# Putting off the last addition of seven units in a dynamic convolution that feeds a maxout layer

## The chip, the core and the metric

The kernel runs on one core of a Trainium2 chip. The metric is the device time of one execution in microseconds (us); the median of three executions stands for the kernel. TensorE (PE) multiplies matrices into PSUM, VectorE (DVE) and ScalarE (ACT) work elementwise, GpSimd (POOL) and SyncE (SP) here mostly issue transfers. Each engine works through its own list of instructions in order, and waits on semaphores for the others.

## What is computed

Two layers follow each other. The first is a convolution whose seven weights are different for every position and head, and are a softmax of an input; the second is a maxout layer with an output projection.

```python
# x: 8 x 4160 x 192, weight_gen: 8 x 4160 x 8 heads x 7 taps
w = exp(weight_gen); w = w / sum(w, axis=-1)          # softmax over the 7 taps
y[b, s, h, :] = sum over k of w[b, s, h, k] * x[b, s - 6 + k, h, :]
# maxout on the 33280 rows of y: w1, w2 192 x 1024, w_out 1024 x 192
out = maximum(y @ w1, y @ w2) @ w_out
```

## The kernel before, in words

**Layout.** The 33280 positions lie as 128 partitions by 260 columns. `BATCHES` are 16 columns each (17 of them, the last of 4). A batch is worked in units: from column 32 on a unit is 8 columns, so batch b has a unit at offset 0 and one at offset 8. A unit is named here by its first column: unit 40 is batch 2, offset 8.

**Softmax.** The weights are exp(w - ln(sum exp w)), so nothing is divided. For each batch: `exp_sum` (ACT, line 162) takes exponents into `e_t`; `red` (DVE, 180) sums over the taps; `ln` (ACT, 186) takes the logarithm; `shift` (DVE, 191) subtracts it from the generated weights in place; `weights` (ACT, 202) takes the exponent again, each value doubled, as bfloat16 in `en_t`.

**Convolution.** For a unit, `mul` (DVE, 218) makes all seven products in one instruction, 128x10752, into its half of the one tile `m_t`. `adds` sums them in three levels: 4608 elements (248), 3072 (254), and the last addition of 1536 (260), which writes `y_t`. Levels two and three read what the level before has written. `beside` is called ahead of each level: on the units at offset 0 it cuts the next batch's `shift` into three parts, on those at offset 8 it puts two halves of a later batch's `red` ahead of levels one and two. Units from column 200 to 239 make the last addition in two halves.

**Around the unit.** `transpose(u)` has SP issue a transposing transfer (273) of `y_t` into `yt`. Results that are ready to be stored (512) are held in a list and issued on SP behind the next transposition. On POOL a copy of one value of `yt` into `gate` (281) makes the queue wait for the transposition; behind it POOL issues loads: for a unit at offset 8 the next x of two batches on and its halo (133, 154), for one at offset 0 the second half of the next batch's x and the weights of three batches on (133, 115).

**Maxout.** max(a, b) is a + relu(b - a), so `hid_tile` (PE, 373) multiplies `yt` by w2 - w1, `relu` (ACT, 383) moves that from PSUM to `rd_t`, and the output is `rd_t` times w_out (PE, 413) plus `yt` times the product of w1 and w_out (PE, 426), both into the same PSUM bank; `evac` (ACT, 498) copies it to `o_t`. Work goes by groups of three tiles (a tile is one eighth of a unit's hidden width), with two or four finished columns to each group in turn. `relay` lets one half of PE's output go behind the other by a wait on ACT's list (476).

**What sets the order.** The order is written out by hand. `hidden` walks a group; `steps` then calls `softmax_steps` and, for each tile, `extra`. `softmax_steps` takes ACT's softmax steps from the table `due`, by tile number; `AT` overrides single entries: ('l', c, 0) is the logarithm of batch c, 'W' are weights, 'X' is `exp_sum`. A step of a long kind can be moved to the next group; a logarithm is done in its group. `extra` has DVE's part: at a batch's tile 0 `mul(b + 1, 0)`, at tile 0 or 5 `adds(b + 1, 0)` with the shift of batch b + 2; at tile 8 `mul(b + 1, 8)`, at 8 or 13 `adds(b + 1, 8)` with the sums of batch b + 3. `wrap_mask` (ACT, 150) clears a part of the halo near the end of the work.

Of the kernel before, what the change touches and what calls it, by code (L numbers as in the profile page):

```python
# [13 lines left out]
ALU = mybir.AluOpType  # L14
# [3 lines left out]
def _sub(base: bass.AP, off: int, dims):  # L18
    ap = [list(base.ap[0])] + [[int(s), int(c)] for s, c in dims]
    return dataclasses.replace(base, offset=base.offset + off, ap=ap)  # L20
# [3 lines left out]
def kernel(  # L24
# [9 lines left out]
    nc = tc.nc  # L34

    B, S, D = x.shape
    H, K = weight_gen.shape[2], weight_gen.shape[3]
    F = moe_w1.shape[1]
    P = 128
# [11 lines left out]
    BATCHES = [(c, min(16, CPP - c)) for c in range(0, CPP, 16)]  # L51
    NB = len(BATCHES)


    def pieces(b):
        n = BATCHES[b][1]
        at, done = [], 0
        for w in (4, 4, 4, 4) if b < 2 else (8, 8) if n == 16 else (n,):
            at.append((done, w))
            done += w  # L60
        return at
# [37 lines left out]
    wg_ts, xb_ts, e_ts, s_ts, en_ts, y_ts, yt_ts = {}, {}, {}, {}, {}, {}, {}  # L99

    m_t = pm.tile([P, K * 16 * D], BF16, name="m_t")
# [20 lines left out]
    def x_at(b, o):  # L122

        c = BATCHES[b][0] + o
        key, at = (b, o) if c < LAST - 8 else ("wrap", 0) if c < LAST else (NB - 2, 8)
        if key not in xb_ts:
            xb_ts[key] = pxb.tile([P, (16 + PAD) * D], BF16, name="xb_t", tag="xb")
        return xb_ts[key], at * D
# [19 lines left out]
    def wrap_mask():  # L148
        halo = xb_ts["wrap"][:, 0:PAD * D]
        nc.scalar.activation(out=halo, in_=halo, func=AF.Copy, scale=msk[:, 0:1])  # L150
# [13 lines left out]
    def part(b, i, of):  # L164

        n = BATCHES[b][1]
        h0, h1 = n * i // of * H, n * (i + 1) // of * H
        return slice(h0, h1), h0 * K, [[K, h1 - h0], [1, K]]
# [4 lines left out]
    def sums(b, hs):  # L173

        at = BATCHES[b][0] * H - (0 if b < FIRST else s_parts[0].shape[-1])
        return s_parts[b >= FIRST][:, at + hs.start:at + hs.stop]

    def red(b, i=0, of=1):
        hs, at, ap = part(b, i, of)
        nc.vector.reduce_sum(out=sums(b, hs), in_=_sub(e_ts[b], at, ap), axis=AX.X)  # L180
# [7 lines left out]
    def shift(b, i=0, of=1):  # L188
        hs, at, ap = part(b, i, of)
        w_t = _sub(wg_ts[b], at, ap)  # L190
        nc.vector.tensor_tensor(out=w_t, in0=w_t, in1=_sub(s_ts[b], hs.start, [[1, hs.stop - hs.start], [0, K]]),  # L191
                                op=ALU.subtract)
# [15 lines left out]
    def mul(b, o):  # L208

        n = dict(pieces(b))[o]  # L210
        t, at = x_at(b, o)
        if n == 4 and b < 2:
            m_out = _sub(m_t, K * o * D, [[64, 2], [P, K * 6], [1, 64]])
            x_in = _sub(t, at, [[2 * D, 2], [D, K], [1, 2 * D]])
        else:
            m_out = m_t[:, K * o * D:K * (o + n) * D]
            x_in = _sub(t, at, [[D, K], [1, n * D]])
        return nc.vector.tensor_tensor(  # L218
            out=m_out, in0=x_in,
            in1=_sub(en_ts[b], o * WGC * 2, [[2, K * n * H], [0, G // 2], [1, 2]]),  # L220
            op=ALU.mult,
        )
# [11 lines left out]
    def in_halves(b, o):  # L234

        return 200 <= BATCHES[b][0] + o < 240

    def adds(b, o, first=False, beside=lambda i, of: None):


        w = dict(pieces(b))[o]
        n = w * D

        def taps(at, step, cnt):
            return _sub(m_t, K * o * D + at * n, [[step * n, cnt], [1, w * D]])

        beside(0, 3)
        nc.vector.tensor_tensor(out=taps(0, 1, 3), in0=taps(0, 1, 3), in1=taps(3, 1, 3), op=ALU.add)  # L248
        if first:
            return  # L250
        beside(1, 3)
        if b not in y_ts:
            y_ts[b] = py.tile([P, 16 * D], BF16, name="y_t", tag="y")
        nc.vector.tensor_tensor(out=taps(0, 2, 2), in0=taps(0, 2, 2), in1=taps(1, 5, 2), op=ALU.add)  # L254
        beside(2, 3)

        of = 2 if in_halves(b, o) else 1
        e = n // 2 // of
        for i in range(of):
            nc.vector.tensor_tensor(  # L260
                out=_sub(y_ts[b], o * D + i * 2 * e, [[64, 2], [P, e // 64], [1, 64]]),
                in0=_sub(m_t, K * o * D + i * e, [[n // 2, 2], [1, e]]),
                in1=_sub(m_t, K * o * D + 2 * n + i * e, [[n // 2, 2], [1, e]]), op=ALU.add,
            )

    def transpose(u):

        b, o, n = UNITS[u]
        yt = pyt.tile([P, 8 // 2 * 3 * P], BF16, name="yt", tag="yt")
        of = 2 if in_halves(b, o) else 1  # L270
        e = n * D // of
        for i in range(of):
            nc.sync.dma_start_transpose(
                out=yt[:, i * e:(i + 1) * e].rearrange("p (b t) -> p b t", t=P),
                in_=y_ts[b][:, o * D + i * e:o * D + (i + 1) * e],
            )
        yt_ts[u] = yt
        while held:
            held.pop(0)()

        nc.gpsimd.tensor_copy(out=gate, in_=yt[:, n * D - 1:n * D])  # L281
        c = b + 1 if o == 0 else b + 2
        if o == 8 and c < NB:
            load_x(c, 0, min(8, BATCHES[c][1]))
        if o == 0 and c < NB and BATCHES[c][1] > 8:
            load_x(c, 8, BATCHES[c][1] - 8)
        if o == 0 and b + 3 < NB:
            load_wg(b + 3, nc.gpsimd)
# [242 lines left out]
    OUTS, c = [[], [], []], 0  # L531
    for g in range(3, len(GROUPS)):
        most = 4 if g == 3 else 2 if GROUPS[g][1] == 2 or len(OUTS[-1]) == 4 else 4
        n = min(most, ready[g] - c)
# [92 lines left out]
    with tc.tile_pool(name="pstage", bufs=1) as pstage:  # L627
# [7 lines left out]
        for at, c, n in ((0, 2, PAD), (PAD, 8, 2), (PAD + 2, 10, 2)):  # L635
            nc.sync.dma_start(
                out=xs[:, at * D:(at + n) * D],
# [83 lines left out]
        for h in range(2):  # L721
# [4 lines left out]
            out=wo[:, :].rearrange("p (f d) -> p f d", d=D),  # L726
# [90 lines left out]
        sum_transpose(3)  # L817
        out_first_weights(OUTS[3])
        adds(1, 4, True)

    pout = work.enter_context(tc.tile_pool(name="pout", bufs=1))
# [8 lines left out]
    def end_of_1():  # L830
        mul(1, 12)
        shift(2)
        adds(1, 12, True)
# [87 lines left out]
    def rest_of_sum(u):  # L921
# [24 lines left out]
        ('l', 11, 0): 144,  # L946
        ('l', 12, 0): 162,
        ('l', 5, 0): 45,
    }
    due = {}  # L950
    for c in range(3, NB):
# [25 lines left out]
    def extra(t):  # L977

        u, k = TILES[t]
        b, o, n = UNITS[u]  # L980
        s = o + k

        if s == 0 and b + 1 < NB:
            mul(b + 1, 0)
        later = 0 if b < 4 else 5
        if s == later and b + 1 < NB:

            c = b + 1
            adds(c, 0, beside=lambda i, of: shift(c + 1, i, of) if c + 1 < NB else None)
        if s == 8 and b == NB - 3:  # L990
            wrap_mask()
        if s == 8 and b + 2 < NB:
            mul(b + 1, 8)
        if s == 8 + later and b + 2 < NB:
            adds(b + 1, 8, beside=lambda i, of: red(b + 3, i, 2) if b + 3 < NB and i < 2 else None)
        if k == n // 4 - 1 and 7 < u + 1 < NU:
            transpose(u + 1)

    def steps(g, tiles):

        if tiles:
            softmax_steps(g)
        for t in tiles:
            extra(t)
# [53 lines left out]
```

## Time and profile before

| | |
|---|---|
| median of 3 runs | 409.7 us (409.62, 409.70, 409.86) |
| the profiled execution | 410.27 us, its span from first to last instruction 408.5 us |
| PE matmul | busy 396.4 us, 97% of the span |
| PE weight load (PEld) | busy 316.5 us, 77% |
| DVE | busy 378.0 us, 93%, 235 instructions |
| ACT | busy 354.8 us, 87% |
| POOL | busy 78.7 us, 19% |
| DVE 218, 128x10752 | 28 times, 5751 ns each |
| DVE 248, 4608 elements | 28 times, 2551 ns each |
| DVE 254, 3072 elements | 28 times, 1752 ns each |
| DVE 260, 1536 elements | 23 times, 955 ns each |
| DVE 191, 280 or 336 values | 26 and 13 times, 444 and 502 ns |
| DVE 180, 448 to 64 values | 24 times, 613 ns |
| transposition, issue to landing | 34 times, median 3.7 us, 2.7 to 5.9 |

A line of the timeline gives the start in us from the span's start, the duration, engine, line and operation, the tile written and those read, and in brackets how long the engine had been idle and what ended that. A line of the chain gives start, length and what was running, followed back from the last instruction to whatever released it. DVE instructions overlap: the next begins some 0.08 us ahead of the end of the one before it, so what an instruction costs its engine is the distance from its start to the next start, not its duration.

### The profile page before, as it was taken

To read this page: it belongs to the slowest core of one execution; us is meant where nothing else is said; L and a number is where in the kernel's file an instruction comes from. 1 tells how busy PE (TensorE), PEld (TensorE's weight loads), DVE (VectorE), ACT (ScalarE), POOL (GpSimd) and SP (SyncE) were. 2 spreads that over 40 slices of the span, in tenths; PEclk is the share of its full clock that TensorE was granted. 3 is DMA by queue.
4 is the path that set the end of the run, shared out by engine and by line. 5 is a ranking of instruction groups with operands and counts; after the bars stand their busy time and mean duration, and the time that the engine had idled before them with its cause. 6 is when DMAs were issued, how large, how long until landed. Compare 5 with 4: busy or idle time off the path is not lost.

```text
span 408.5 us, 16132 instructions
## 1 busy us (share of the span) xinstructions
PE 396.4 (97%) x7369; PEld 316.5 (77%) x7369; DVE 378.0 (93%) x235; ACT 354.8 (87%) x420; POOL 78.7 (19%) x108
## 2 busy tenths in 40 slices
PE   7799999999999999999999999999999999999994
PEld 2589899777778777777877787777778777877794
DVE  6999999999999999999999999999999999999400
ACT  4889899999999988998989999899998899898771
POOL 1420122121212201222221122212212213110000
PEclk9999999999999999999999999999999999999999
DMA  8995588665767656775765676587468577936313
GB/s 252 251 196 139 153 151 198 146 159 153 194 92 230 187 109 140 219 190 107 219 183 105 161 207 181 106 215 192 100 161 214 142 107 220 178 80 155 116 66 119
DMA packets 65270, 66.32 MB, mean 162 GB/s; under 512 B 49585, under 2 KB 54321, under 8 KB 65200
## 3 DMA queue, kind: packets, MB, share of 16 engines
q1 hardware_dynamic: 56224, 40.54, 36.2%
q0 software_dynamic: 8832, 24.63, 29.8%
q8 instruction: 58, 0.95, 0.9%
q10 hardware_dynamic: 144, 0.10, 0.1%
q14 instruction: 12, 0.10, 0.1%
HBM read 37.33 MB, written 25.56 MB: 154 GB/s over the span
## 4 chain that ended last, share of the span: by engine, by line
PE 70%; DVE 17%; ACT 5%; DMA 3%; issue 1%; SPq 1%; POOL 0%; DVEq 0%; ACTq 0%; POOLq 0%
PE op_ps L413 31%; PE hd L373 29%; DVE m_t L218 8%; PE op_ps L426 6%; DVE m_t L248 4%; ACT rd_t L383 3%; DVE m_t L254 3%; PE hdp L373 2%; DMA ws1T<-in_moe_w_dram 2%; PE yps L318 2%; DVE y_t L260 1%; DMA xb_t<-in_x_dram 1%; DMA yt<-y_t 1%; DVE wg_t L191 1%; DVE s_rest L180 1%
## 5 line engine op out<-in xcount | busy, mean ns | idle before, releaser
L383 ACT ACTIVATE rd_t<-hd 128x1024 bf16<-128x1024 f32 (+1 forms) x206 | 234.5, 1188 | 26.0 <-PE hd L373 24.7
L413 PE MATMUL op_ps<-wo,rd_t 64*128 64x192 bf16 x4160 | 210.6, 243 | 0.1
L413 PEld LDWEIGHTS <-rd_t 64*128 64x128 bf16 x4160 | 180.8, 94 | 15.7 <-issue 0.3
L373 PE MATMUL hd<-yt,wd 64*128 64x512 bf16 (+1 forms) x1584 | 187.3, 360 | 0.4 <-ACT rd_t L383 0.3
L218 DVE TENSOR_TENSOR m_t<-xb_t,en_t 128x10752 bf16<-128x10752 bf16 (+1 forms) x35 | 181.5, 5192 | 0.1
L373 PEld LDWEIGHTS <-wd 64*128 64x128 bf16 x1776 | 94.2, 94 | 44.6 <-issue 4.0
L281 POOL CAST gate<-yt 128x1 f32<-128x1 bf16 x29 | 39.5, 1361 | 260.0 <-DMA yt<-y_t 260.0
L248 DVE TENSOR_TENSOR m_t<-m_t 128x4608 bf16<-128x4608 bf16 (+1 forms) x31 | 75.5, 2436 | 0.1
L498 ACT COPY o_t<-op_ps 128x384 f32<-128x384 f32 (+1 forms) x99 | 57.1, 588 | 12.5 <-PE op_ps L413 12.5
L426 PE MATMUL op_ps<-w,yt 64*128 64x192 bf16 x768 | 54.6, 243 | 0.1
L426 PEld LDWEIGHTS <-yt 64*128 64x128 bf16 x768 | 37.7, 94 | 16.3 <-issue 1.0
L254 DVE TENSOR_TENSOR m_t<-m_t 128x3072 bf16<-128x3072 bf16 (+1 forms) x29 | 50.0, 1724 | 0.1
L202 ACT ACTIVATE en_t<-wg_t 128x896 bf16<-128x896 f32 (+2 forms) x45 | 35.9, 820 | 0.2 <-DVE wg_t L191 0.2
L260 DVE TENSOR_TENSOR y_t<-m_t 128x1536 bf16<-128x1536 bf16 (+1 forms) x34 | 27.6, 825 | 0.5
L133 POOL DMA_DIRECT2D xb_t<-in_x_dram x34 | 18.3, 538 | 31.7 <-ACT rd_t L383 20.7
L191 DVE TENSOR_TENSOR wg_t<-wg_t,ln_t 128x280 f32<-128x280 f32 (+5 forms) x46 | 22.2, 482 | 0.4 <-ACT ln_t L186 0.3
L383 ACT ACTIVATE rd_t<-hdp 128x1024 bf16<-128x1024 f32 x16 | 16.3, 1037 | 1.6 <-PE hdp L373 1.6
L162 ACT ACTIVATE e_t<-wg_t 128x896 f32<-128x896 f32 (+2 forms) x18 | 16.3, 903 | 1.4 <-DMA wg_t<-in_weight_gen_dram 1.4
L488 DVE COPY o_last<-op_ps 128x192 f32<-128x192 f32 x1 | 0.4, 358 | 18.1 <-ACT o_last L488 18.1
L180 DVE TENSOR_REDUCE s_rest<-e_t 128x64 f32<-128x448 f32 (+2 forms) x27 | 16.3, 604 | 0.0
L373 PE MATMUL hdp<-yt,wd 64*128 64x256 bf16 x192 | 13.8, 270 | 2.3 <-ACT rd_t L383 2.0
L318 PE MATMUL yps<-ident,m_t 64*128 64x64 bf16 x600 | 12.1, 190 | 1.1 <-issue 0.6
(54 smaller groups left out, 88.6 us busy)
## 6 DMA issues: line engine op xcount, KB each, us to landing
out_dram<-o_t SPq DMA_DIRECT2D x22, 768.0 KB, 4.9
xb_t<-in_x_dram POOLq DMA_DIRECT2D x30, 384.0 KB, 5.0
out_dram<-o_t SPq DMA_DIRECT2D x20, 384.0 KB, 3.1
wg_t<-in_weight_gen_dram POOLq DMA_DIRECT2D x13, 448.0 KB, 5.8
xb_t<-xb_t POOLq DMA_DIRECT2D x15, 288.0 KB, 5.2
xb_t<-in_x_dram POOLq DMA_DIRECT2D x4, 192.0 KB, 5.9
xs<-in_x_dram SPq DMA_DIRECT2D x1, 576.0 KB, 3.7
yt<-y_t SPq DMA_TRANSPOSE x34, 3.7
```

Source lines behind the costliest of these rows:

```text
L191: nc.vector.tensor_tensor(out=w_t, in0=w_t, in1=_sub(s_ts[b], hs.start, [[1, hs.stop - hs.start], [0, K]]), op=ALU.subtract)
L202: nc.scalar.activation(out=_sub(en_ts[b], (o * WGC + j * N * K) * 2, [[2 * N, K], [2, N], [1, 2]]), in_=_sub(wg_ts[b], (o * H + j * N) * K ...
L218: return nc.vector.tensor_tensor(out=m_out, in0=x_in, in1=_sub(en_ts[b], o * WGC * 2, [[2, K * n * H], [0, G // 2], [1, 2]]), op=ALU.mult,)
L248: nc.vector.tensor_tensor(out=taps(0, 1, 3), in0=taps(0, 1, 3), in1=taps(3, 1, 3), op=ALU.add)
L254: nc.vector.tensor_tensor(out=taps(0, 2, 2), in0=taps(0, 2, 2), in1=taps(1, 5, 2), op=ALU.add)
L260: nc.vector.tensor_tensor(out=_sub(y_ts[b], o * D + i * 2 * e, [[64, 2], [P, e // 64], [1, 64]]), in0=_sub(m_t, K * o * D + i * e, [[n // ...
L281: nc.gpsimd.tensor_copy(out=gate, in_=yt[:, n * D - 1:n * D])
L373: nc.tensor.matmul(hid_out(t, f, j), lhsT=wd_at(j, s, f // 4, f % 4 * P, P), rhs=_sub(yt_ts[u][half(j), :], (s + j) % 3 * P, [[3 * P, w // ...
L383: relu_of[t0] = nc.scalar.activation(out=rd[:, k * 1024:(k + n) * 1024], in_=hd[:, at:at + n * 1024], func=AF.Relu)
L413: return nc.tensor.matmul(op_out(c), lhsT=rd[half(r), k * 1024 + at:k * 1024 + at + P], rhs=wo[half(r), f * D:(f + 1) * D], start=start, s ...
L426: nc.tensor.matmul(op_out(c + j), lhsT=yt_ts[u][half(j), (3 * i + (s + j) % 3) * P:(3 * i + (s + j) % 3 + 1) * P], rhs=w10[half(j), s * D: ...
L498: nc.scalar.copy(out=_sub(o, c % 24 * D, [[D, len(qs)], [h * D, 2], [1, D]]), in_=_sub(tile_, at + (qs[0] - p) * D, [[D, len(qs)], [512, 2 ...
```

## The change

For the seven units named in `PUT_OFF`, `adds` does not issue the last addition but keeps it in a list; `last_add`, called right behind each `mul` in `extra`, issues it behind the next unit's product. The places at which `beside` puts parts of `shift` or `red` change with it. Place 0 (between product and first addition) falls away where a put-off addition now stands there; place 2 (ahead of the last addition) falls away where the unit's own last addition is put off. The step is cut into as many parts as there are places left. Three logarithms, of batches 10, 14 and 15, are listed one group sooner, at tiles 127, 193 and 208 instead of 130, 196 and 212.

```diff
+    PUT_OFF = (32, 40, 48, 64, 72, 80, 88)
+    last_adds = []
+
+    def put_off(b, o):
+        return BATCHES[b][0] + o in PUT_OFF
+
-    def adds(b, o, first=False, beside=lambda i, of: None):
+    def adds(b, o, first=False, beside=lambda i, of: None, after=False):
...
-        beside(0, 3)
+        places = [i for i, there in enumerate((not after, True, not put_off(b, o))) if there]
+
+        def beside_at(i):
+            if i in places:
+                beside(places.index(i), len(places))
+
+        beside_at(0)
         nc.vector.tensor_tensor(out=taps(0, 1, 3), in0=taps(0, 1, 3), in1=taps(3, 1, 3), op=ALU.add)
...
-        beside(1, 3)
+        beside_at(1)
...
         nc.vector.tensor_tensor(out=taps(0, 2, 2), in0=taps(0, 2, 2), in1=taps(1, 5, 2), op=ALU.add)
-        beside(2, 3)
...
+        beside_at(2)
+
+        def last():
+            of = 2 if in_halves(b, o) else 1
...
+        if put_off(b, o):
+            last_adds.append(last)
+        else:
+            last()
+
+    def last_add():
+        if last_adds:
+            last_adds.pop()()
...
+        ('l', 15, 0): 208,
+        ('l', 14, 0): 193,
+        ('l', 10, 0): 127,
...
             mul(b + 1, 0)
+            last_add()
...
-            adds(c, 0, beside=lambda i, of: shift(c + 1, i, of) if c + 1 < NB else None)
+            adds(c, 0, beside=lambda i, of: shift(c + 1, i, of) if c + 1 < NB else None, after=put_off(c - 1, 8))
...
             mul(b + 1, 8)
+            last_add()
...
-            adds(b + 1, 8, beside=lambda i, of: red(b + 3, i, 2) if b + 3 < NB and i < 2 else None)
+            adds(b + 1, 8, beside=lambda i, of: red(b + 3, i, min(of, 2)) if b + 3 < NB and i < 2 else None,
+                 after=put_off(b + 1, 0))
```

More of the change, by code (lines that the diff above doesn't have):

```diff
@@ L254, in adds @@
         nc.vector.tensor_tensor(out=taps(0, 2, 2), in0=taps(0, 2, 2), in1=taps(1, 5, 2), op=ALU.add)
-        beside(2, 3)
[L257 to L264, printed above, removed]
+        beside_at(2)
+        def last():
+            of = 2 if in_halves(b, o) else 1
+            e = n // 2 // of
+            for i in range(of):
+                nc.vector.tensor_tensor(
+                    out=_sub(y_ts[b], o * D + i * 2 * e, [[64, 2], [P, e // 64], [1, 64]]),
+                    in0=_sub(m_t, K * o * D + i * e, [[n // 2, 2], [1, e]]),
+                    in1=_sub(m_t, K * o * D + 2 * n + i * e, [[n // 2, 2], [1, e]]), op=ALU.add,
+                )
+        if put_off(b, o):
[5 more added lines that the diff above has]
+            last_adds.pop()()
     def transpose(u):
```

## The prediction, made before the changed kernel was run

> **What bounds the kernel now.** I read PE's waits first, then the chain that ended last, and then the periods in the timelines. The waits of PE, in us in total, times, longest:
>
> ```profile
> PE hdp L373 <- ACT rd_t L383: 2.0, 3, 0.9
> PE warm L689 <- DVE ident L666: 1.6, 1, 1.6
> PE warm L689 <- DVE m_t L227: 0.7, 1, 0.7
> ...
> PE hd L373 <- ACT rd_t L383: 0.3, 1, 0.3
> PE warm L709 <- DVE wd L704: 0.3, 1, 0.3
> ```
>
> All of PE's waits for DVE are on lines of the opening, before 12.5 us. The change touches nothing before the subtraction at 47.15. Behind that PE never waits for DVE. Now the chain around the place where it leaves PE (start, length):
>
> ```profile
> 254.88 1.32 PE op_ps L413 x32
> ...
> 263.52 1.32 PE op_ps L413 x32
> ...
> 272.15 1.32 PE op_ps L413 x32
> ...
> 278.15 5.75 DVE m_t L218
> ...
> 348.56 1.29 SPq L273
> 349.94 3.43 DMA yt<-y_t
> 353.50 1.03 POOL gate L281
> 354.53 3.47 DMA xb_t<-in_x_dram
> 358.21 1.26 ACT xb_t L150
> ...
> 367.33 1.32 PE op_ps L413 x32
> ```
>
> The chain runs over DVE from 278 to 348, and that looks as if DVE set the end. PE's own beat says otherwise. The block of 32 matmuls comes back every 8.64 us (263.52 less 254.88; 272.15 less 263.52). From 272.15 to 367.33 are 95.18 us; eleven beats of 8.635 are 94.99. In the whole stretch that the chain gives to DVE, PE loses 0.2 us. Starts of single matmuls in the trace confirm it: from 48 us to the last group the only distances over 0.21 us are 0.51 at 79.25 (PE there waits for ACT; 0.06 is normal at this step), 0.43 at 360.75, and four of about 0.25, where 0.20 is normal. So PE bounds the kernel, with some 0.9 us of gaps behind 48 us.
>
> DVE is busy without a gap from 41 to 355 us but is not late. I counted 48 hidden matmuls a unit and set the first of each against the landing of its transposition: for units 32, 40, 48, 64, 72, 80, 88 `yt` lands 10.1, 10.5, 9.8, 8.3, 7.4, 7.6, 7.2 us before its use. The lead shrinks as DVE takes 23.67 us for 16 columns (products at 41.49 and 65.15) and PE 23.03 (16/6 of 8.635), down to 1.2 us at units 216 and 232, and never to nothing.
>
> **The change part by part.** The row lengths are distances from start to next start on DVE.
>
> Ten instructions go, as the lists of the two built kernels show (248 rows, 238 now). Subtraction: parts of 280, 280 and 336 cost 0.36 + 0.36 + 0.42 = 1.14; two of 448 cost 2 x 0.54 = 1.09 (row at 15.87, next start 16.41); one of 896 costs 1.01 (38.22 to 39.23). Units 32, 64 and 96 go from three parts to two, 3 x 0.05 = 0.15. Units 48 and 80 go to one part, 2 x 0.13 = 0.26. Sums: two halves cost 1.06 (58.97 to 59.50, twice), one whole 1.00 (40.49 to 41.49); units 40, 72, 88: 3 x 0.06 = 0.18.
>
> The second saving is a stall between two additions of which one reads the other:
>
> ```profile
> 50.34 1.75 DVE L254 TENSOR_TENSOR m_t<-m_t 128x3072 bf16<-128x3072 bf16 x1
> 52.01 0.50 DVE L191 TENSOR_TENSOR wg_t<-wg_t,ln_t 128x336 f32<-128x336 f32 x1
> ...
> 62.49 1.75 DVE L254 TENSOR_TENSOR m_t<-m_t 128x3072 bf16<-128x3072 bf16 x1
> 64.28 0.96 DVE L260 TENSOR_TENSOR y_t<-m_t 128x1536 bf16<-128x1536 bf16 x1
> ```
>
> With a subtraction behind it line 254 costs 1.67, with its reader right behind it 1.79. The 0.12 goes at units 40, 72, 88 (the next product stands there) and 56 (a half sum does): 4 x 0.12 = 0.48. DVE gains 0.15 + 0.26 + 0.18 + 0.48 = **1.07 us**, all of it by about 146 us.
>
> What this is worth to the end: PE waits for DVE nowhere, so nothing directly. The one place left is 0.24 us at 360.75 (0.43 less 0.20), where ACT is late because of `wrap_mask`. The profile says that the mask waited 0.19 us for a load that DVE's chain had delayed. But its own list says:
>
> ```profile
> L150 ACTq EVENT_SEMAPHORE  x3: 38/38/38, 358.0 to 358.1; - x3
> ```
>
> Three waits stand ahead of the mask, each 38 ns, minimum and maximum alike: none of them was held. They begin behind the relay of line 476, which PE releases at 357.87, and three steps of 0.076 are the 0.19. An earlier load moves nothing there: **0**.
>
> The delayed last addition. It now follows the next product (5.67 us to the next start), less what DVE has saved till then: `y_t` comes 5.6 us later at unit 32, 5.4, 5.3, 5.1, 4.9, 4.8 at the next five, 4.6 at 88. Leads of 10.1 to 7.2 us become 4.5 at unit 32, 3.2 at 64, 2.5 at 72, 2.6 at 88. The cover holds unless a landing grows by 2.5 us; the slowest in the trace took 5.9 against a median of 3.7, which is 2.2 more. Cost 0, bounds 0 and (2.5 us beyond the cover) what rival B works out; nothing can be gained here. On SP the stores held behind a transposition go with it, some 2 us late at most; the stores next issued are ready at 56.30, 69.64, 81.02 and 105.42, the transpositions now at about 59.0, 70.7, 82.4 and 105.9. `o_t` holds 24 columns, and a place comes round again after 24 columns, over 30 us: nothing waits.
>
> POOL's gate. It is a copy on POOL and does not get through while a product runs:
>
> ```profile
> 69.36 1.59 POOL L281 CAST gate<-yt 128x1 f32<-128x1 bf16 x1 [8.62 <-DMA yt<-y_t]
> ...
> 80.88 1.89 POOL L281 CAST gate<-yt 128x1 f32<-128x1 bf16 x1 [8.91 <-DMA yt<-y_t]
> ```
>
> The first ends at 70.95, the product that ran ends at 70.91; the second at 82.77, its product at 82.72. A gate that came during a sum over taps took 0.19 (153.78). In the changed order a transposition that lands 3.7 us behind its issue meets the second addition, and the gate ends with that one: about 64.1, 75.8, 87.0, 110.9, 122.5, 134.2, 146.1, some 4.5 us later than before. What is queued behind it on POOL: the x loads have 12 us and more until their product. The weight loads of batches 5 to 8 landed at 65.97, 90.42, 115.82, 136.54 and their exponents began on ACT at 76.90, 95.73, 122.52, 148.43: 10.9, 5.3, 6.7, 11.9 ahead. Less 4.5 the least is 0.8, with the slow landing of 7.2 us that this load had. No cost.
>
> [...]
>
> Logarithms. DVE comes 1.07 us earlier; those of batches 10, 14 and 15 ended 0.93, 0.67 and 1.25 us ahead of their subtraction (211.89 and 212.82; 306.89 and 307.56; 330.11 and 331.36), so as listed before two of them would have held DVE. A group sooner they end about 3 to 6 us earlier, behind their sums (204.58, 299.24, 323.05 less 1.07). ACT issues as many as before; 0.21 us moves to another group. The same pairing, logarithm then weights, stands at 113.88 and 114.09, and PE shows no gap there: 0, bounds plus and minus 0.2. The next tightest, weights of batch 11 (253.13 for a product at 254.49), has 1.36 against 1.07.
>
> **Sum.** The profiled execution took 410.27 (span 408.5 and 1.77 around it), 0.57 over the median. 410.27 - 0 = 410.27 in its terms, **409.7** for the median.
>
> **The rivals.**
>
> A, faster: DVE does pace the end, as the chain has it from 278 to 348, and the 1.07 us come off: 409.7 - 1.07 = 408.6. Against it stands the 0.2 us that PE lost there. [...] The beat of 8.64 speaks against it. 6%.
>
> B, slower: a gate does not get in between the second addition and the next product, which begins 0.08 us before the addition ends, or its transposition lands more than 4.9 us behind the issue. It then waits out a product, 5.7 us more. Place: units 64 to 88. At unit 64 the loads would go at 116.6 and 117.1; the weights land 5.8 (median) to 8.9 us (that load's row) later, 122.9 to 126.0, and the exponent due at 122.52 holds ACT, its relus and PE for 0.4 to 3.5. At unit 88 loads issued at 140.0 and 140.5 would run beside a transposition issued at 140.9; landing when they do (146.3 to 149.4) it would miss the use at 147.33 by up to 2.1. I take 1.1: 410.8. It decides at a landing 4.9 us behind the issue. For it: 4 of the first 9 transpositions took 4.5 to 5.9. Against it: the gate did get in at product and subtraction, which overlap by the same 0.08 us. 14%.
>
> C, a little: the mask did wait for its load, and 0.19 us go: 409.5. The three equal waits speak against it. 10%.
>
> **How the numbers follow.** Forecast 70%, 409.7. The kernel's measurement can tell about 0.2%, 0.8 us. Forecast and C lie within that: 80%; A is faster, 6%; B slower, 14%. The range 409.2 to 410.6 takes in forecast and C with the 0.2 us of the logarithms, and B's lower half.
>
> **What would show it.** DVE with 225 instructions; product of unit 240 at about 1.07 us before 348.80; that of unit 248, at 359.91, now waiting up to 0.6 for the mask, which stays near 358.2; gates at the seven times above; PE's beat 8.64 throughout and 0.43 again near 360.75. A gate near 116.6, or an exponent that waits for a load, means B; a gap gone at 360.75, C; a shorter beat after 272, A. A PE wait for `yt` in units 64 to 88 would make the prediction wrong.

## The result

The changed kernel takes 430.03 us (median of six executions, 426.93 to 431.11) where the kernel before took 410.13 beside it: a ratio of 1.0473, 95% interval 1.0435 to 1.0511. The profiled execution took 429.94 us, 19.7 more than that of before (spans 428.2 and 408.5). Line numbers from 248 on have moved: 248 is now 261, 254 is 267, 260 is 274, 273 is 296, 281 is 304, 373 is 396, 383 is 406, 413 is 436, 426 is 449, 476 is 499.

**Where it is lost.** First the slices of the span, 10.7 us each:

```profile
PE   7799999599999982999999999999999999999994
...
DVE  5999999599869966899999999999999999999500
...
POOL 1420209316901580222212212112212213130000
PEclk9999999879999995999999999999999999999999
```

PE has two holes, in the 8th slice (75 to 86 us) and the 16th (161 to 171), and the granted clock falls at both (digits 8 and 7 in the 8th and 9th slice, 5 in the 16th). DVE, which was full before, has holes as well. POOL, whose digits were 0 to 2 there, shows three blocks with peaks of 9, 9 and 8. From the 18th slice on the rows look as they did before: the beat in the chain (179.46, 188.09, 196.72, 205.36) is still 8.63 to 8.64 us. First uses of each unit's `yt` by PE come 7.45 us later at unit 48 (98.05, before 90.60), 7.9 at unit 88, 19.56 at unit 96 (178.63, before 159.07), and 19.55 for the rest. So 7.5 us go near 80, 0.4 on the way and 11.6 near 165.

The waits (us in total, times, longest):

```profile
ACT e_t L162 <- DMA wg_t<-in_weight_gen_dram: 19.1, 3, 12.6
...
PE op_ps L436 <- ACTq L499: 13.4, 2, 9.9
...
DVE m_t L218 <- DMA xb_t<-in_x_dram: 9.3, 2, 4.7
...
DVE m_t L218 <- DMA xb_t<-xb_t: 5.3, 1, 5.3
...
PE hd L396 <- ACT rd_t L406: 1.8, 1, 1.8
```

PE waits for ACT, ACT's exponents wait for the generated weights, and DVE's products wait for x. The chain tells in what order that came about, around the first hole (start, length):

```profile
59.46 3.75 DMA yt<-y_t
63.21 0.05 issue
63.27 11.55 POOL gate L304
...
76.69 5.10 DMA wg_t<-in_weight_gen_dram
...
81.82 0.02 ACT e_t L162
...
82.68 1.92 ACT rd_t L406 x2
84.60 0.04 issue
84.64 2.75 PE hd L396 x12
```

Read from the top: the transposition of unit 32 lands at 63.21; POOL's copy into `gate` begins and does not end; the load of batch 5's weights behind it is issued only at 76.69 and lands 5.1 us later; the exponent, the relus behind it and PE follow. The copy itself, and DVE at that time:

```profile
63.27 12.96 POOL L304 CAST gate<-yt 128x1 f32<-128x1 bf16 x1 [11.67 <-DMA yt<-y_t]
76.17 0.53 POOL L133 DMA_DIRECT2D xb_t<-in_x_dram  x1
76.69 0.55 POOL L115 DMA_DIRECT2D wg_t<-in_weight_gen_dram  x1
```

```profile
62.77 1.75 DVE L267 TENSOR_TENSOR m_t<-m_t 128x3072 bf16<-128x3072 bf16 x1
64.43 5.75 DVE L218 TENSOR_TENSOR m_t<-xb_t,en_t 128x10752 bf16<-128x10752 bf16 x1
70.10 0.95 DVE L274 TENSOR_TENSOR y_t<-m_t 128x1536 bf16<-128x1536 bf16 x1
70.97 2.55 DVE L261 TENSOR_TENSOR m_t<-m_t 128x4608 bf16<-128x4608 bf16 x1
73.44 1.08 DVE L191 TENSOR_TENSOR wg_t<-wg_t,ln_t 128x896 f32<-128x896 f32 x1
74.44 1.75 DVE L267 TENSOR_TENSOR m_t<-m_t 128x3072 bf16<-128x3072 bf16 x1
80.77 5.76 DVE L218 TENSOR_TENSOR m_t<-xb_t,en_t 128x10752 bf16<-128x10752 bf16 x1 [4.58 <-DMA xb_t<-in_x_dram]
```

A copy of one value a partition takes 12.96 us. It comes during a second addition, and five two-input instructions later, at 76.19, DVE has nothing to run: its next product (80.77) wants the x load that is queued behind the copy. 0.04 us later the copy ends. The copies of units 56 (99.80, 13.59 us) and 80 (143.54, 13.83 us) go the same way: that of 56 ends with the addition ahead of a sum over taps, that of 80 when DVE again has to wait for x.

At the second hole the weights of batch 8 go at 157.82 and take 11.03 us to land, beside two x loads and a transposition; their exponent waits 12.6 us and PE about 10. Behind the holes PE's matmuls stand about twice as far apart as usual (those of line 396 behind the first one 0.397 us where 0.197 is normal), and the granted clock is down: 0.50 from 84 to 89 us and from 162 to 171, 0.72 in the mean of either stretch of the changed kernel below (columns: stretch, length, busy us of PE, PEld, DVE, ACT and POOL, PEclk, DMA share, GB/s); the first fence is the kernel before:

```profile
80.00:92.00 12.00, 12.00 (x208) 9.23 (x206) 11.97 (x7) 11.03 (x14) 2.90 (x3) 1.00 0.58 140
...
157.00:175.00 18.00, 18.00 (x317) 14.04 (x314) 17.96 (x11) 16.31 (x19) 2.75 (x3) 1.00 0.78 207
```

```profile
80.00:92.00 12.00, 8.19 (x104) 6.22 (x106) 11.23 (x6) 7.30 (x8) 0.95 (x2) 0.72 0.57 156
...
157.00:175.00 18.00, 8.05 (x120) 6.01 (x116) 11.22 (x6) 6.08 (x7) 4.61 (x9) 0.72 0.73 114
```

Of the first 7.45 us, 5.5 are waits (distances of 3.88 and 2.04 less two normal ones of 0.2), and I put the other 1.9 down to the slow clock; of the 11.6 at the second, 10.0 and 1.6. The granted clock went to half near 83 us, behind the distance of 3.88, and near 162, inside one of 10. In the run of section 5 below, the granted clock was at half from 96.6 to 100.0 us (0.92 in the mean from 80 to 100) with nothing longer before it than distances of 0.88, 1.19 and 1.40 us between matmuls, within 4.5 us; there it took no single gap of 3.88 us.

DVE itself is as forecast: 225 instructions, 377.6 us busy (378.0 before).

### The profile page after: what moved, and what is told of

The parts are those of the page before. It is cut to its first block, busy times and chain, and to the rows that moved or that the text cites. A ratio compares the mean times of both kernels' runs of the same rounds, so it can differ in the third digit from the quotient of the medians.

```text
span 428.2 us, 16124 instructions
## 1 busy us (share of the span) xinstructions
PE 400.6 (94%) x7369; PEld 318.7 (74%) x7369; DVE 377.6 (88%) x225; ACT 354.9 (83%) x420; POOL 112.1 (26%) x108
## 4 chain that ended last, share of the span: by engine, by line
PE 67%; DMA 10%; DVE 7%; issue 6%; ACT 5%; POOL 3%; SPq 1%; ACTq 0%; DVEq 0%; POOLq 0%
PE op_ps L436 30%; PE hd L396 28%; PE op_ps L449 6%; DVE m_t L218 4%; DMA wg_t<-in_weight_gen_dram 4%; DMA yt<-y_t 3%; ACT rd_t L406 3%; POOL gate L304 3%; DMA xb_t<-xb_t 2%; PE hdp L396 2%; DMA ws1T<-in_moe_w_dram 2%; PE yps L341 1%; DVE m_t L261 1%; DVE m_t L267 1%; ACT o_t L521 0%
## 5 line engine op out<-in xcount | busy, mean ns | idle before, releaser
L304 POOL CAST gate<-yt 128x1 f32<-128x1 bf16 x29 | 73.2, 2523 | 240.2 <-DMA yt<-y_t 240.2
L191 DVE TENSOR_TENSOR wg_t<-wg_t,ln_t 128x280 f32<-128x280 f32 (+5 forms) x39 | 21.1, 541 | 0.4 <-ACT ln_t L186 0.3
```

## The experiments

The theory after the result, T1: POOL's copy reads SBUF and is kept out while DVE runs long two-input instructions without a break; all else follows from the late loads. The rivals: the put-off addition itself makes `yt` late; the merged subtractions and sums alone are enough; the logarithms; transfers that collide.

### 1. No copy, in the changed kernel and in the one before

```diff
-            nc.sync.dma_start_transpose(
+            turn = nc.sync.dma_start_transpose(
...
-        nc.gpsimd.tensor_copy(out=gate, in_=yt[:, n * D - 1:n * D])
+        tc.add_manual_dep(nc.gpsimd.nop().ins, turn.ins.name, SYNC, reason="loads behind the transposition")
```

> The changed kernel, but POOL no longer copies a value of yt: its first load behind a transposition waits for the transposition itself, so POOL reads nothing from SBUF. Theory 1 (the copy is shut out while DVE runs two-input instructions back to back; the weight loads behind it come late, their exponents hold ACT, and ACT holds PE): the three 13-us copies are gone, the loads of batches 5 and 8 are issued some 13 us sooner, no exponent waits over 1.5 us, and the time falls from 430.0 to 409.0 to 411.0. Theory 2 (the put-off addition itself makes yt late for PE): stays above 420. Theory 3 (transfers get in each other's way as soon as additions and loads are shifted against each other): between 412 and 425.

Measured: 409.87 us, ratio to the kernel before 0.9999 (0.9988 to 1.0009). The whole loss is gone with an edit that leaves every put-off addition, every merged part and every logarithm where the change put them. PE's row of 157 to 175 us is full again, at full clock:

```profile
157.00:175.00 18.00, 18.00 (x324) 14.19 (x320) 17.96 (x10) 16.34 (x19) 1.22 (x3) 1.00 0.96 228
```

The later additions do shorten the leads of `yt`: 5.5, 4.5, 3.6, 2.4, 2.5, 2.0 and 0.8 us at units 32, 40, 48, 64, 72, 80 and 88. None is used up, so the rival of the late `yt` falls. That of colliding transfers falls with the time, which it put at 412 or more.

> The kernel before with the same edit, as a control: loads come about 1.3 us sooner than behind the copy. Theory 1: the cover there was enough, so within 0.5 us of the kernel before, 409.3 to 410.3. If the copy cost something in the kernel before as well: 406 to 409. If loads that come sooner run into the transpositions: 411 or more.

Measured: 410.03 us, 1.0003 (0.9993 to 1.0013). In the kernel before the copy costs nothing, and its absence is worth nothing.

### 2. The logarithms, and the merging, alone

The first is the kernel before with the three new entries of `AT`; the second is the changed kernel with `last()` called at once in place of the branch on `put_off`.

> The kernel before with nothing but the three logarithms one group sooner. Theory 1: no part in the loss, 409.5 to 410.3. Rival (a logarithm that comes ahead of relus pushes ACT and PE): 411 to 413 and new waits of PE for ACT near 180, 277 and 300 us.

Measured: 409.82 us, 0.9989 (0.9978 to 1.0000): nothing lost.

> The changed kernel with nothing put off: each last addition at once, but subtractions and sums in the fewer parts and places of the change. Theory 1 (it takes the put-off additions): the copies end with the product that they meet, since the addition behind it has to wait for it; 409.3 to 410.5. Rival (fewer parts are enough, as fewer sums and subtractions open the way): copies of 10 us and more, 415 to 430.

Measured: 410.82 us, 1.0014 (0.9997 to 1.0032). No copy lasted over 1.9 us. Fewer sums and subtractions are not enough; it takes the put-off additions.

### 3. A small instruction at the boundary

```diff
         if put_off(b, o):
+            nc.vector.reduce_sum(out=spare, in_=ident[:, 0:64], axis=AX.X)
             last_adds.append(last)
```

> The changed kernel with a sum over 64 values of a constant (some 0.13 us on DVE) behind the second addition of each of the seven units. It gives DVE one one-input instruction ahead of each next product. Theory 1 in its form 'an instruction with one input opens the way': the copies of units 32, 56 and 80 end with the second addition, at about 64.6, 104.5 and 144.9, and the time is 409.5 to 411.5. If so short a sum does not let the copy in: three copies of 13 us again and 428 to 432. Theory 2: 430, whatever the copies do.

Measured: 409.56 us, 0.9996 (0.9977 to 1.0015). Seven instructions of 0.21 us that compute nothing anyone reads take back 20 us. The copy of unit 32 and what follows it on POOL:

```profile
63.25 1.08 POOL L305 CAST gate<-yt 128x1 f32<-128x1 bf16 x1 [12.12 <-DMA yt<-y_t]
64.27 0.53 POOL L133 DMA_DIRECT2D xb_t<-in_x_dram  x1
64.80 0.55 POOL L115 DMA_DIRECT2D wg_t<-in_weight_gen_dram  x1
```

It ends 0.05 us behind the second addition, where the prediction had it. Not every copy was free: those of units 56 and 88, which came ahead of other boundaries, took 3.4 and 7.2 us, and that cost nothing. But what about the small sum opens the way? I took it to be its single input. Two controls at the same place:

> As the run with the small sum, but the seven small instructions behind the second additions are additions of two inputs of 64 values. If it is the one input of the small sum that opens the way for POOL's copy: the copies of units 32, 56 and 80 are shut out for 13 us as in the changed kernel, 427 to 432. If any short instruction or one more boundary does: they end near 64.6, 104.5 and 144.9, and 409.5 to 411.5.

Measured, one execution: 411.01 us (its neighbours of the kernel before: 409.50 to 411.57). The copy of unit 32 took 1.35 us. My reading was wrong: an addition of two inputs opens the way too, if it is that short.

> The same place, a copy of 64 values in bfloat16: one input, but no sum. One input is enough: the copies of POOL end with the second additions, 409.5 to 411.5. Only a sum opens the way: 427 to 432.

Measured, one execution: 409.44 us, copies as in the run with the sum. Then the length:

> As the run with the small addition of two inputs of 64 values, now 256. It costs DVE some 0.2 us a piece. If a short instruction opens the way whatever its inputs, and 256 is still short: no copy over 4 us behind the second additions of the seven units, 409.5 to 412. If what counts is that the instruction is only some 0.1 us long: copies of 10 us and more again, 415 to 432.

Measured, one execution: 428.64 us.

```profile
64.06 13.40 POOL L305 CAST gate<-yt 128x1 f32<-128x1 bf16 x1 [11.33 <-DMA yt<-y_t]
77.41 0.53 POOL L133 DMA_DIRECT2D xb_t<-in_x_dram  x1
```

> The same with 1024 values, some 0.65 us a piece and so as long as a subtraction of 448 or as the put-off addition, behind which copies stayed shut out. If only short instructions open the way: copies of 10 us and more, 415 to 435. If any additional instruction at this place does: no copy over 4 us, 410 to 413.

Measured, one execution: 430.36 us, the copy of unit 32 14.0 us long. So an instruction of 64 values (0.09 to 0.13 us from start to start) let the copy in all six times that one was waiting there, in each of the three runs, even where the copy had already been passed over twice (unit 56). With 256 values (0.20 us) and with 1024 the copies of units 32 and 48 were held 11.8 to 14.0 us, and of the copies that met a second addition with the small instruction behind it only those of 64 and 72 got in at once.

### 4. Reading, or any access

```diff
-        nc.gpsimd.tensor_copy(out=gate, in_=yt[:, n * D - 1:n * D])
+        tc.add_manual_dep(nc.gpsimd.memset(gate, 0.0).ins, turn.ins.name, SYNC, reason="loads behind the transposition")
```

> POOL's copy replaced by a memset of the gate tile behind the same transposition: POOL writes SBUF but reads nothing. If it is the read that is shut out: no memset over 0.3 us, 409.3 to 410.6. If any access of POOL to SBUF is: memsets of 10 us and more, 415 to 432.

Measured: 410.43 us, 0.9999 (0.9983 to 1.0016). The group of the memsets (min, median and max in ns):

```profile
L304 POOL MEMSET gate<- x29: 99/99/100, 62.8 to 379.3; 128x1 f32 x29
```

Not one of 29 was held, through products and additions alike. It is the read: beside the same row of two-input instructions a copy that reads `yt` took up to 13.83 us, a memset that only writes 0.099. And the wait is longer than the instruction that the copy met: in the changed kernel the copy of unit 32 was out until 76.2, past that addition (end 64.5) and past the product behind it (70.2).

### 5. Which late load costs the time

The load of weights is put ahead of the copy; x stays behind it:

```diff
+        if o == 0 and b + 3 < NB:
+            load_wg(b + 3, nc.gpsimd)
         nc.gpsimd.tensor_copy(out=gate, in_=yt[:, n * D - 1:n * D])
...
-        if o == 0 and b + 3 < NB:
-            load_wg(b + 3, nc.gpsimd)
```

> The changed kernel with the load of weights issued ahead of the copy instead of behind it and the x load; x loads stay behind the copy. The copies should still last 13 us at units 32, 56 and 80. Theory 1a (the late weight loads are the whole loss, through ACT's exponents): no exponent waits over 1.5 us, 409.5 to 412. Theory 1b (the x loads, late by the same copies, would hold the products on DVE and so PE by themselves): DVE waits of 4.6, 5.3 and 4.7 us as in the changed kernel sum to 14.6, against a lead of some 2.6 us at unit 88, so about 12 us are lost, 420 to 424, and PE waits for yt instead of for relus.

Measured: 424.15 us, 1.0332 (1.0307 to 1.0356). The copies still last 13 to 14 us, no exponent waits over 1.4 us, and 14 us are lost nevertheless:

```profile
DVE m_t L218 <- ACT o_t L521: 5.6, 1, 5.6
DVE m_t L218 <- DMA xb_t<-xb_t: 4.9, 1, 4.9
DVE m_t L218 <- DMA xb_t<-in_x_dram: 4.9, 1, 4.9
PE hd L396 <- DMA yt<-y_t: 4.1, 4, 2.0
```

DVE's products wait 15.4 us for x (the first line names ACT, but that product began at 82.06, right behind the x load that landed at 81.97), and then PE waits for `yt`. So the copies hit PE on two roads. The road over x alone costs 14 of the 20 us; what the road over ACT would cost alone no run shows. In the changed kernel the two are about equally long between the holes: `yt` of units 72, 80 and 88 landed there 0.15, 0.04 and 0.13 us ahead of its use.

### 6. Fewer put-off units, and the old places

> The changed kernel with only units 32, 48, 64 and 80 put off, so that no two neighbours are. Between second addition and next product there is now a sum or a subtraction and the unit's own last addition, at every second unit. Theory 1 (it takes a long run of two-input instructions, which only two neighbours put off make): no copy over 6 us, 409.5 to 411. If a single put-off addition is enough: copies of 10 us and more, 415 or above.

Measured: 420.61 us, 1.0261 (1.0240 to 1.0283). The branch of the theory missed, and the other one, that a single put-off addition is enough, came true. The copies of units 40 and 72 were held, 12.1 and 10.9 us. POOL around the first:

```profile
63.21 0.64 POOL L304 CAST gate<-yt 128x1 f32<-128x1 bf16 x1 [12.10 <-DMA yt<-y_t]
63.80 0.53 POOL L133 DMA_DIRECT2D xb_t<-in_x_dram  x1
64.32 0.55 POOL L115 DMA_DIRECT2D wg_t<-in_weight_gen_dram  x1
73.02 12.11 POOL L304 CAST gate<-yt 128x1 f32<-128x1 bf16 x1 [8.15 <-DMA yt<-y_t]
```

The put-off unit 32 gets in. Unit 40, which is not put off, is shut out: its transposition, issued at 65.28 while the two loads at 63.80 and 64.32 were running, landed at 72.90, 7.6 us later where the kernel before needed 4. The copy so missed the product and met the first addition behind it. That the two loads slowed the transposition is read from this coincidence; no run moves the loads alone. One put-off neighbour is enough for a long run.

> The seven last additions put off, but subtractions in three parts and sums in two halves at the places of the kernel before. Behind a product now come the put-off addition and then a subtraction of 280 values or a half sum. The copy of unit 32 meets the second addition of unit 40 and the product behind it. Theory 1 with 'a short subtraction opens the way as it did behind a product in the kernel before': that copy ends at about 71, the weights land at 76.5, some 410 to 412. Theory 1 with 'no two-input instruction opens it': shut out until the half sum near 84, more than 20 us, and 430 to 440.

Measured: 421.84 us, 1.0291 (1.0262 to 1.0320). The copy of unit 32 lasted 13.2 us, that of 64 13.0. Neither 'a short subtraction opens the way' (it passed three of 280 to 336 values) nor the full price of the other branch: DVE ran dry at 76.7, for want of x, before the half sum could come.

### 7. One copy freed at a time

The small sum of section 3 at one unit only.

> The changed kernel with the small sum behind the second addition of unit 40 only, so that the copy of unit 32 is free and those of 56 and 80 are not. If the stalls add (7.5 us from the copy of unit 32, 0.4 and 11.6 from that of unit 80): 429.9 less 7.5, 421 to 423. If the loss is set by how late the weights of batch 8 land, and the first stall was swallowed by that: DVE is only 4.6 us earlier, the weights land near 164 where they are due at 148.4, some 15 us are lost, 423.5 to 427.

Measured: 420.03 us, 1.0218 (1.0184 to 1.0252), below both expectations. With unit 32 freed, the later copies met other boundaries: shut out were now 40 (10.3 us) and 64 (13.0), while 56 and 80 got in after 0.3 and 1.3 us. A sum of stalls can't be read from such a run.

> The small sum behind the second addition of unit 88 only: the copy of unit 80 is free, those of units 32 and 56 are not. If the stalls add: 429.9 less 11.6, 417.5 to 419. By the x loads the same: DVE waits 4.6 and 5.3 us for them, less a lead of 2.5 us at unit 72 is 7.4, 416.5 to 418.5. If the copy of unit 56 costs nothing and that of 32 less than it seems: 413 to 416.

Measured: 419.6, 419.9, 428.3 and 429.3 us in four executions, too far apart for a ratio; the profile is of the first. In it unit 80 is freed, 32 and 56 are shut out for 13.0 and 13.5 us, and the time is 0.6 us over the range that adding gave. What the two long executions did no trace shows, so this one tells little.

### What decides at a boundary

Take every end of a two-input instruction of DVE at which a copy was waiting and behind which DVE ran on without a stop, over all 14 traces with a copy. If a sum or an instruction of 64 values came next, the copy got in every time (ahead of a sum 11 of 11 in the kernel before and 11 of 11 in the changed one). If a two-input instruction of over 0.4 us came next, it depended on how the copy had met it. A copy that began to wait in a product got in at its end 114 times of 116; the other two began in its last 0.1 us and got in one instruction later. One that began in an addition got in 13 times of 37, in a subtraction 8 of 10. One that had missed its first boundary in any other way got in at none of the 93 that it met afterwards; it waited for a sum, for one of the small instructions, or for DVE to stand idle.

The pair of instructions does not tell which way it goes: the same second addition and product, with the same overlap of 0.08 us, shut out unit 32 at 64.51 and let in unit 72 at 133.04.

```profile
121.27 5.76 DVE L218 TENSOR_TENSOR m_t<-xb_t,en_t 128x10752 bf16<-128x10752 bf16 x1 [5.27 <-DMA xb_t<-xb_t]
...
131.28 1.75 DVE L267 TENSOR_TENSOR m_t<-m_t 128x3072 bf16<-128x3072 bf16 x1
132.95 5.75 DVE L218 TENSOR_TENSOR m_t<-xb_t,en_t 128x10752 bf16<-128x10752 bf16 x1
```

```profile
131.97 1.11 POOL L304 CAST gate<-yt 128x1 f32<-128x1 bf16 x1 [14.91 <-DMA yt<-y_t]
```

What does tell in the traces is DVE's last stop, a place where an instruction began behind the end of the one before it instead of 0.08 us ahead. Count from the instruction behind the stop. Where the one that ended was among the first six, the copy got in 136 times of 138 (the other two are those of the last 0.1 us); where it was the seventh or a later one, once in 120. At unit 72 above it was the fifth, at unit 32 the 17th. This also takes the two hits away from the runs with 256 and 1024 values: their copies of 64 and 72 met the fifth instruction behind a stop. The 64-value additions opened the way up to the 48th.

The kernel before has such a stop in every batch, 0.03 us long: its last additions at 64.28, 87.94, 111.61 and 135.28 wait for the second addition right ahead of them. The changed kernel has none of these; between 31 and 162 us DVE stops only at 80.77 and 121.27, for x. The run with nothing put off has 14 between 52 and 143. This is read from the traces. No run changes the stops alone, the traces cannot tell the count from the time since the stop (in up to 11.8 us, out from 12.7 us on), and why a stop should matter stays open.

## Why the prediction was wrong

- **The step that failed**: "In the changed order a transposition that lands 3.7 us behind its issue meets the second addition, and the gate ends with that one: about 64.1, 75.8, 87.0, 110.9, 122.5, 134.2, 146.1". The landings were right (63.2 for unit 32), and with the small sum in place the copies ended at 64.3, 76.1, 87.5, 111.5, 123.3 and 135.1 at the first six of the seven. In the changed kernel 48, 64 and 72 did end with a second addition; 32 and 80 were held 12.96 and 13.83 us, and so was 56, which is not put off and so was not on the list (13.59). With the small sum the seventh, unit 88, ended at 153.5 in place of 146.1. The row that it was drawn from, product and subtraction, tells of a product that was the second instruction behind a stop of DVE (the addition at 64.28).
- **What the change took out with it**: "The second saving is a stall between two additions of which one reads the other", four times 0.12 us, was booked as gain alone. These stalls are the stops of the section above.
- **Rival B had the mechanism and not its size.** It named the boundary and put the weights that are loaded behind unit 64 in danger, but let the copy wait out "a product, 5.7 us more" and took 1.1 us for the end. The lock-out was 13 to 14 us, over six to eight instructions with the one that the copy met, and the end 19.7. It also watched units 64 to 88 only; of the loss, 7.5 us come from unit 32. The 0.8 us of lead that were reckoned for the weights rested on the failed step. Given 14%, it should have been followed to the point where DVE meets its next sum or runs dry.
- **"The x loads have 12 us and more until their product"**: true, and used up. The products waited 4.6, 5.3 and 4.7 us for x, and by the run with weights ahead that alone costs 14 us.
- **Right**: PE bounds the kernel and DVE's saving is worth nothing. Without the copy the product of unit 240 began at 347.69 against 348.80, 1.11 us sooner (1.07 forecast), and the time was 0.9999 of before. So rival A falls. The put-off additions cost nothing, with leads of 2.4 and 2.5 at units 64 and 72 (3.2 and 2.5 forecast), though 0.8 at 88 (2.6). The logarithms cost nothing. C falls too: the gap of 0.43 us is still there without the copy, at 359.95.

The forecast of 409.7 is what the change gives with the copy out of the way (409.87, 409.56, 410.43).

## What to carry to other kernels

An instruction that is there only to pace a queue need not read SBUF on POOL. Here such a read beside long two-input instructions of DVE cost 19.7 us, while a wait on the semaphore in its place (409.87 us) or a memset, which writes and doesn't read (410.43), cost nothing. When a change takes sums, idle time or dependent stalls out of a row of two-input DVE instructions, list every POOL read that falls into the row and follow it to the next sum, 64-value instruction or stop of DVE (13 to 14 us here), not to the next boundary (5.7 us in rival B). And where one stall delays several loads, look for the second road behind the first: with the weights loaded ahead of the copy, the x loads still cost 14 us of the 20.

## What was not expected of the hardware

A one-value copy on POOL was kept out for 13.83 us in the changed kernel, and for 14.0 with additions of 1024 values in it, by DVE instructions of at most 5.8 us, while a memset of the same tile took 0.099 us all 29 times. A 64-value instruction of DVE (a sum, a copy or an addition of two inputs; 0.09 to 0.13 us) opened the way all six times that a copy was waiting there, in each of three runs; that a 256-value one of two inputs, 0.07 us longer, did so no trace shows. At a boundary between long two-input instructions a copy got in where DVE had stopped shortly before (136 times of 138 at the first six instructions behind the stop, once in 120 at later ones), and a stop of 0.03 us was enough. A transposition issued 1 to 1.5 us behind two loads took 7.6 us, where that of the kernel before took 4.0.
